# A kernel whose whole order is a table of words: the same steps in another order

## The chip, the cores and the metric

The kernel runs on one core of a Trainium2 chip. Five engines work side by side, each strictly in its own order: TensorE (PE; its weight loads are a row of their own, PEld), VectorE (DVE), ScalarE (ACT), GpSimd (POOL), and SyncE (SP), which here only issues transfers to the 16 DMA engines. The metric is the time of one execution on the device in microseconds (us). Three runs of the kernel before gave 236.62, 237.85 and 238.53 us; the median is 237.85.

## The reference

Two stages in a row, in float32 at the outside. The first is attention over 8 batches, 8 heads, 576 tokens and 64 numbers a head: a coarse attention over means of four tokens, and a local one in a band of three tokens to each side. The second mixes tokens and channels.

```python
q_d = q.reshape(B, H, Sd, factor, D).mean(axis=3)      # k_d, v_d likewise; factor 4
out_up = np.repeat(sm_attn(q_d, k_d, v_d), factor, axis=2)
mask = np.abs(pos[:, None] - pos[None, :]) < factor
out_local = softmax(where(mask, scale * q @ k.T, -1e9)) @ v
x = out_up + out_local                                  # as [batch, token, 512]
theta = x @ w_theta
zr, zi = x * cos(theta), x * sin(theta)
y = einsum('ts,bsd->btd', w_tok_r, zr) + einsum('ts,bsd->btd', w_tok_i, zi)
u = x + y
return u + maximum(u @ w_ch, 0.0)
```

## The kernel before

Batches run one behind the other, but several are under way at once: while one batch is mixed over its tokens, the next is in its attention, and the loads of later ones are on their way. Every batch goes through steps with names of two letters, and a step is a few instructions on one engine.

- Loads, issued by SP into 16 staging slots of 128 x 576 float32: lk and lq (two heads of k or q each, L287), lv and lw (two halves of a v chunk, 64 rows with 256-byte pieces, L348), la, lb, lc (theta, token and channel weights, L240 to L257). ck, cq, cv, ca, cb and cc cast them to bfloat16 (L296, L396, L243, L261).
- Attention: tp transposes q and k on PE (L303), ev brings them from PSUM (L316), kd and qd are sums of four tokens (L322 to L336). pv and vd make the coarse v (L404, L412, L415). sd, ed, nd, xn, xd and xc are the coarse attention. ps are the local scores (L482), ex their exponentials (L490), mk the band (L501), po the product with v (L511), nm the division (L519, L520), xt the turn to channels by tokens (L533), xa the sum with the coarse part into xT (L541).
- Mixing: th and tt are theta (L552, L564), cs and ct its cosine and sine on ACT (L557 to L570), xm turns x back (L591), zz multiplies (L616), zt with zp and zc or with a transposing transfer dz handles the last 64 tokens. mx multiplies by the token weights, nine products for each of eight pieces of a batch (L632), and ua adds x (L637). The token weights themselves are transposed once on PE (wp, L273) and brought back (wc, L278).
- Output: ch is the channel product (L662), up and uc, or the transposing transfer du (L641), turn u to tokens by channels, rl adds and clips (L667), st stores (L671). The last 64 tokens of two batches go together: ut, dt, ht, rt, and the tail stores ss and sr (L700).

For batches 6 and 7 the transposes xm are transfers too (dx, L601), and for batch 7 those of k and q (dk, L307).

What sets the order is one long string, ORDER (L57 to L97). Each word is the next step of its kind; the letters behind the name are the place: a PSUM bank or pair of banks, a staging slot, or the engine of a cast or an eviction (v DVE, a ACT, g POOL). A word wm is a stretch of warm-up products (L755), on zeros, whose result nobody reads. te and ts load ACT's tables. The loop at L749 walks the string, and pin() ties each instruction to the one ahead of it on its engine, so each engine's order, SP's queue included, is the string's:

```python
for word in ORDER.split():
    kind, place = word[:2], word[2:]
    ...
    STEPS[kind][0](*next(todo[kind]), place)
    pin()
```

Waits between engines follow from the data: a step waits for what it reads, for its bank, slot or buffer to be free, and a load also for the landing of the eighth load ahead of it.

Of the kernel before, what the change touches and what calls it, by code (L numbers as in the profile page):

```python
# [58 lines left out]
lq9 x11 tp45 kcg cqa cva cqg x16 cqg lka cvv cvv lqb evv cvv ckg cva lkc kdg cka cqa lqd ckg lke laf wm772 tp23 evv
wm754 tp67 pv45 tp01 qdv kcg eva vdv la0 kdg lq1 eva cka wm256 ps23 ex ps67 lk2 qdv ps01 mkv wm446 sd45 sd23 ex ed  # L60
po67 ed cav cqg la3 po45 nm nm lk5 nd67 cqa xn mkg nd23 ex xn cag cka tp45 lq6 eva la4 po01 po67 lb8 nm lb9 xd2 wm303
tp45 lb7 cqa lba lqb ckg lbc lbe xcv mkg lbd lbf xt01 caa nm lb1 po23 kdg xa eva lv0 lv2 xt67 tp45 lw cag th0 lv5 cba
cbg lw cbg cqg lw xa xm1 nm th6 xt23 lv6 evv th7 ts cs xa zz tp45 cbg cbg wp0 cs wcv lv3 xm6 cs tt2 xm3 th7 wp1 lw xm0
zz zz lw qdv lk8 wcv eva ct lk4 lq9 cs cbg cbg cbg cbg wp6 wca wp3 wp2 wp4 wp5 wca wp1 wcv wcv wcv wp2 ztg ps67 ps45
qdg wcv te ex wcv ex lq7 kdg lkb lka zz lkc lqe lkd zp1 zcv cvv lqf mx3 cvg cvg cvg mkv ua cvg lq1 mx2 sd01 ps67 lv0
mkv lq2 ex po45 mx3 nm sd67 ua cqg po45 ed lw po01 nm ua nm mx2 ed ua pv67 po45 lq5 mx3 cqg vda nm nd01 ua cka up2
nd67 mkg cka xn ckg ckg lk6 uca xn up3 tp45 uca tp01 xd6 eva ckg xt23 mx7 xcv eva qdg xa xt45 po01 th6 cqg xa lv3 ckg
lv9 tp23 nm ts cs cqa th4 lq7 xm5 xt01 th6 evv cs tp23 xa zz cqa tt4 ua tp01 kdg cs ct cqg evv ztv th5 lw evv lw xm7
zz cs tp23 mx6 xm4 kdg zp5 qdg ua eva zz cvv ps01 cqa ps23 lv8 xm7 kdg zz zcv lk4 te ex lw mx6 mx4 ua mx5 sd01 mkv lvb
lw ua ex po67 mkv cva ps23 qdg lca lcc utg ed lce nm mx4 cvg ex lcd lvf ua lk1 po01 lk2 sd67 lw po23 ckg nm cqa nm mx5  # L70
ckg ed tp01 cvg ua lq5 eva tp67 mx4 lq0 cca ua up5 evv cvg ua ccg ccg pv23 mkg ucv vda lk3 qdv ps01 ps67 ex up4 mx5
ccv nd23 ex ua nd01 uca kdg ch5 po67 xn ps23 ckg cka lv9 mx4 xn tp01 lw ex mkg rl nm lk6 cva ckg xd5 sd23 ua cqg xcv
xt67 lv7 eva mx4 lw lv4 lw cvg xa lv8 lw ed xt01 po23 po67 th5 ua ch4 cqa ts cs xa nm nm th0 po23 lqb xt67 rl up1 cs
nm kdg th5 xm0 xa cs xm4 tp23 xm6 tt7 mkg cvg zz th0 lqc ucv zz st up1 cvg up5 ch4 eva ucv ckg ct ucv ch1 zz po23 cs
sd67 lve lva rl mkv te ed cvg pv45 lqd lk1 ztg cqg ch0 rl rl lk2 ch1 qdg nm lq3 vda tp67 nd45 rl cqa xm0 lqf eva lw zz
xn nd23 zp1 utg lw xn tp67 zca lk5 lq9 kdg mx0 up1 ua po45 lv0 eva ckg lk7 ps23 nm lw po67 nm ckg lv4 uca mx0 tp45 lk6
qdg mx1 ua xd0 ps67 ua lv8 ex eva xca ckg sd23 xt45 xa lw mx1 mkg st cvg ua ed mx0 ex mx1 mkv ua th0 po23 ua xt45 ts
cs xa xt67 mx1 xm0 xa th4 xm5 lqb zz ua tt0 kdg xm1 cvv ckg cvv th6 ch7 cqg cka cqg cs ct nm cs lvc cqg lk1 ztv tp23
eva lw th0 rl zz cs cqg zz tp67 evv cvg xm4 zz st zp5 zca ch1 rl cva tp23 mx0 po67 ua eva ps45 lw nm po23 lv2 te ex
lv5 mx1 pv67 lke cqg st mx0 po45 dt vda nm lk7 mkv st lqd po23 ckg ua ua qdg sd67 ch1 qdg nm nm ht0 cka ed rt lv3 up6  # L80
up7 cvg ucv uca nd45 kdg cqg nd23 mx0 xn lw xn ps67 ss ps45 ex ex xd2 mx3 tp67 xcv up2 cva ua uca tp45 lq6 rl evv up0
cqg lw eva ch1 ua lvf xt67 ps23 ucv sd45 xa cva st ex lw lq9 rl lk4 mx0 sd23 ed xt67 ua ckg xa lva qdg lw mkv kdv xt45
mx1 cvg th0 ua st lvb mx6 ua lw ed mkg tp23 ts cs utg lw mx7 cqg xa ua up6 po01 po45 cvg eva uca pv23 tt7 nm vda lq0
nm th6 xm0 zz nd45 ct cs ch1 lv1 xn cva st tp23 nd67 cva xn up0 th4 xm5 th6 zz sr eva xm7 xm5 ps23 lv8 lvc rl uca cs
po01 ch4 zz lw cs nm zz ztg ch7 te ex dz xd6 ch5 cvg rl lw lqe utg rl mkg po01 ps23 st mx4 lw lkd up7 cqg cka st ex
up2 uca nm ch3 rl xt01 kdg st st cvg xcv cva qdg ckg ua xa mkg uca po45 pv67 mx2 nm mx0 ua lk6 sd45 vda lk2 rl lq7
xt67 cqg ua ps23 xa mx1 lv5 ed po45 ua lq3 nm st mkv cqg dt ex dk9 sd23 xt67 ckg ed mx0 mkg du xa nd45 ch1 ckg ua po23
xn po67 th0 ts cs th4 tt5 nm cs nd23 rl dkf nm ct cqg evg dka xm1 xm0 mx6 zz th1 th7 cs dk1 cs xm4 xm5 zz ztv xn ua zz
mx6 zz mx4 po23 ua dz xt01 po67 xd5 ua xcv eva lw evg mx4 nm st mx5 eva du xa mx2 ht3 qdg ua mx4 xt01 ua kdg nm ua utg
ps67 du rt cvv du st ps23 kdg ua te ex ex mx5 mx4 ps67 lvb lv0 lw lw qdv xa lv8 sd23 cva xt01 ua mkv xa mkg mx5 ex st  # L90
lv4 ua po67 ua ed nm sd01 ed po23 mkg cvg ch4 ch5 mx0 nm tt1 lw lw cvg cvg rl sr po67 rl dxd po23 ua nm po45 nm ts ct
nm th0 pv67 th1 dx vda ch2 ztg nd45 st st nd67 du xn du xn cs cs du th3 cs th0 xd1 xt45 xt67 rl xcv cs xt23 xa utg dxc
ch1 dx zz ch0 ch4 xa ss ch5 dz th6 zz ch7 dt du xa tt2 zz th3 dxe dx zz st cs rl th1 mx6 cs mx3 ct st ua rl ztv rl cs
dx7 dx mx2 th6 ht4 rt zz mx1 ua mx0 cs rl mx3 mx6 zz dz rl zz ua ua zz mx7 mx1 mx2 ua ua mx0 ua mx3 ua mx6 ua ua mx1
st ua du mx0 st mx2 ua ss utv ch3 ua ua ua st ua utv ch2 ch1 ch0 ch7 ch6 du ch4 du du du du st rl sr rl du du rl dt
ch1 st st rl st rl st st rl rl ht0 rl st st rm su rt sr ss st
# [702 lines left out]
```

## Time and profile before

| What | Value |
|---|---|
| time, median of three runs | 237.85 us (236.62 to 238.53) |
| span of the profiled execution, first to last instruction | 232.1 us |
| mean granted TensorE clock in it | 0.997 |
| DMA queue of the program, share of 16 engines | 84.6% |
| bytes moved, mean rate | 49.41 MB, 213 GB/s |

For the profiled execution the page gives the span alone; what lies around a span is in the runs' times and not in the page. Its busy table gives each engine's busy time, its share and its instructions. The slices cut the span in 40 equal parts of 5.8 us; a digit is the busy share in tenths. Rows of a group read: line, engine, operation, out<-in, size, count | busy us, mean ns of one | idle us ahead of them and who ended it. Rows of the timeline begin with start and duration in us. Rows of waits read: who waited <- for whom: us in total, times, longest.

### The profile page before, as it was taken

The page shows a single profiled execution, that of the slowest core. Times are in us where ns is not written, and L with a number is a line of the kernel's source. Part 1 is how long each engine was busy: PE and PEld are TensorE (multiplying, and loading weights), DVE is VectorE, ACT ScalarE, POOL GpSimd, SP SyncE. Part 2 cuts the span into 40 slices and gives each one's busy share as a digit, 9 for nine tenths or more (in the row PEclk, how much of TensorE's full clock was granted, in tenths as well). Part 3 has the DMA queues.
Part 4 walks back from the last instruction along what each step waited for, and adds up shares of the span by engine and source line. Part 5 has one row for each costly group of instructions (what it writes and reads, how often), then busy time and mean ns, then how long its engine had stood idle before and what let it go on. Part 6 is the DMA issues. An engine that isn't in the chain of part 4 may idle for free.

```text
span 232.1 us, 9462 instructions
## 1 busy us (share of the span) xinstructions
PE 220.7 (95%) x3986; PEld 153.2 (66%) x3986; DVE 191.8 (83%) x365; ACT 156.1 (67%) x241; POOL 135.5 (58%) x179
## 2 busy tenths in 40 slices
PE   7998899999998999999999999999999998999991
PEld 2665678777776765776768766676676563767750
DVE  6699999989997988868997997799889967567572
ACT  3359999799877989867976979857766591620000
POOL 7468989869999656897472837767386510000000
PEclk9999999999999999999999999999999999999998
DMA  6999989999999899989606895899957766556676
GB/s 204 382 392 390 298 134 252 365 263 193 264 263 195 224 290 208 203 209 210 174 3 178 226 234 147 293 249 173 153 122 189 144 138 100 154 126 182 138 235 217
DMA packets 76795, 49.41 MB, mean 213 GB/s; under 512 B 61136, under 2 KB 61392, under 8 KB 76752
## 3 DMA queue, kind: packets, MB, share of 16 engines
q1 hardware_dynamic: 76752, 48.81, 84.6%
q8 instruction: 31, 0.51, 1.1%
q14 instruction: 12, 0.10, 0.2%
HBM read 33.98 MB, written 9.44 MB: 187 GB/s over the span
## 4 chain that ended last, share of the span: by engine, by line
PE 72%; DVE 12%; DMA 5%; SPq 3%; issue 3%; ACT 2%; DVEq 0%
PE PS L632 24%; PE PS L662 10%; PE PS L552 9%; PE PS L303 5%; PE PS L755 4%; PE PS L511 3%; DVE xT L541 3%; DMA out_dram<-osb 2%; DVE pm L501 2%; PE PS L591 2%; PE PS L482 2%; DMA st<-xT 2%; SPq L641 2%; PE PS L533 2%; DVE uT L637 2%
## 5 line engine op out<-in xcount | busy, mean ns | idle before, releaser
L632 PE MATMUL PS<-WT,z 128*128 128x288 bf16 x576 | 77.9, 286 | 1.7 <-issue 1.7
L632 PEld LDWEIGHTS <-z 128*128 128x128 bf16 x576 | 53.8, 98 | 17.5 <-issue 2.8
L637 DVE TENSOR_TENSOR uT<-PS,xT 128x288 bf16<-128x288 f32 x64 | 28.1, 450 | 11.4 <-PE PS L632 11.1
L552 PE MATMUL PS<-wth,xT 128*128 128x512 bf16 x128 | 32.3, 380 | 0.7 <-DVE xT L541 0.7
L557 ACT ACTIVATE cs<-PS,pihc 128x512 bf16<-128x512 f32 x32 | 22.3, 696 | 15.1 <-PE PS L552 9.9
L662 PE MATMUL PS<-wch,uT 128*128 128x512 bf16 (+1 forms) x132 | 30.6, 373 | 0.0
L520 DVE TENSOR_TENSOR tmp<-PS,rl 128x512 bf16<-128x512 f32 x40 | 27.7, 692 | 1.4
L541 DVE TENSOR_TENSOR xT<-PS,xdT 128x928 bf16<-128x928 f32 (+1 forms) x24 | 22.7, 952 | 3.4 <-PE PS L533 3.1
L490 ACT ACTIVATE pm<-PS 128x1024 bf16<-128x1024 f32 (+1 forms) x24 | 20.4, 877 | 7.0 <-PE PS L482 2.7
L501 POOL TENSOR_TENSOR pm<-pm,band 128x1024 bf16<-128x1024 bf16 (+1 forms) x13 | 22.2, 1709 | 2.9 <-ACT pm L490 2.9
L667 DVE SCALAR_TENSOR_TENSOR osb<-PS,ur 128x512 f32<-128x512 f32 (+1 forms) x33 | 21.8, 669 | 2.4 <-PE PS L662 1.6
L330 POOL TENSOR_TENSOR two<-kT 128x580 f32<-128x580 bf16 x15 | 17.5, 1163 | 6.1 <-ACT kT L316 5.2
L296 POOL CAST q_tm<-st 128x576 bf16<-128x576 f32 x22 | 14.4, 664 | 10.8 <-DMA st<-in_q_dram 10.8
L662 PEld LDWEIGHTS <-uT 128*128 128x128 bf16 x132 | 12.2, 98 | 12.2 <-issue 0.3
L558 ACT ACTIVATE cs<-PS 128x512 bf16<-128x512 f32 x32 | 19.4, 605 | 0.0
L330 POOL TENSOR_TENSOR two<-qT 128x576 f32<-128x576 bf16 x11 | 12.8, 1167 | 10.5 <-ACT qT L316 7.1
L552 PEld LDWEIGHTS <-xT 128*128 128x128 bf16 x128 | 11.2, 98 | 10.7 <-issue 1.3
L616 DVE TENSOR_TENSOR z<-PS,cs 128x1024 bf16<-128x1024 bf16 x24 | 16.2, 685 | 1.9 <-PE PS L591 0.9
L437 ACT ACTIVATE pd<-PS 128x864 bf16<-128x864 f32 x16 | 14.1, 889 | 5.2 <-PE PS L426 5.2
L761 ACT ACT_TABLE_LOAD x13 | 16.7, 1283 | 0.2
L296 POOL CAST k_tm<-st 128x576 bf16<-128x576 f32 x21 | 14.4, 695 | 1.4 <-DMA st<-in_k_dram 1.4
L396 POOL CAST v_w<-st 128x512 bf16<-128x512 f32 x21 | 13.3, 653 | 1.3 <-DMA st<-in_v_dram 1.2
(119 smaller groups left out, 419.3 us busy)
## 6 DMA issues: line engine op xcount, KB each, us to landing
st<-in_q_dram SPq DMA_DIRECT2D x32, 288.0 KB, 6.3
st<-in_k_dram SPq DMA_DIRECT2D x32, 288.0 KB, 6.0
st<-in_v_dram SPq DMA_DIRECT2D x70, 128.0 KB, 4.7
out_dram<-osb SPq DMA_DIRECT2D x31, 256.0 KB, 2.9
out_dram<-osb SPq DMA_DIRECT2D x10, 128.0 KB, 2.4
st<-in_v_dram SPq DMA_DIRECT2D x4, 288.0 KB, 3.7
st<-in_moe_w_tok_r_dram SPq DMA_DIRECT2D x4, 288.0 KB, 6.2
st<-in_moe_w_tok_i_dram SPq DMA_DIRECT2D x4, 288.0 KB, 7.2
```

Source lines behind the costliest of these rows:

```text
L296: COPY[w](out=to[:, r, :], in_=of[:, r, :])
L330: nc.gpsimd.tensor_tensor(out=t, in0=src[:, :, 0:2], in1=src[:, :, 2:4], op=ALU.add)
L490: nc.scalar.activation(out=pm[(3 * b + u) % NPM][:, :, 0:n].rearrange("p e c j w -> p e (c j w)"), in_=at.pop(("ps", b, u))[:, :, 0:4 * W ...
L501: EW[w].tensor_tensor(out=t, in0=t, in1=m, op=ALU.mult)
L520: nc.vector.tensor_tensor(out=tmp[(NCH * b + c) % NTMP].rearrange("p g (j d) -> p g j d", d=D), in0=ps[:, :, :, 0:D], in1=r.unsqueeze(3).t ...
L541: nc.vector.tensor_tensor(out=xT[b % 2][:, :, lo:lo + cnt].rearrange("p e (m j) -> p e m j", j=4), in0=at.pop(("xt", b, u))[:, :, 0:cnt].r ...
L552: nc.tensor.matmul(out=ps, lhsT=xT[b % 2][:, dc, P * c:P * c + P], rhs=wth[:, dc, :], start=(dc == 0), stop=(dc == 3))
L557: nc.scalar.activation(out=t[:, 0, :], in_=ps, func=AF.Sin, bias=pihc, scale=1.0)
L632: nc.tensor.matmul(out=ps, lhsT=z[b % 2][:, j, P * dc:P * dc + P], rhs=WT[:, j, cols], start=(j == 0), stop=(j == 8))
L637: nc.vector.tensor_tensor(out=uT[b % 2][:, dc, cols], in0=at.pop(("mx", b, i)), in1=xT[b % 2][:, dc, cols], op=ALU.add)
L662: nc.tensor.matmul(out=ps[:, cols], lhsT=uT[b % 2][:, dc, P * c:P * c + P], rhs=wch[:, dc, cols], start=(dc == 0), stop=(dc == 3))
L667: nc.vector.scalar_tensor_tensor(out=o[:, cols], in0=at["ch", b, c][:, cols], scalar=0.0, in1=ur[b % 2][:, c, cols], op0=ALU.max, op1=ALU.add)
```

## The change

All of ORDER is replaced, and nothing else. It has the same steps in another sequence, with other banks, slots and engines. The word k0, which does nothing, goes to the end. A line of the difference as an example, and the table's first line in both forms:

```diff
@@ -55,45 +55,45 @@
 ORDER = """
-l10 l11 l12 c1v c1a c1g k0 l13 kcv wm061 t101 c1g lq4 e1v wm256 t123 lk5 lk6 kca e1v wm483 x12 x13 lk7 ckv lq8 x10 cka
...
+l10 c1a l11 c1g l12 l13 wm7a5 t101 c1v c1v t123 lk4 kcg ckv lk5 lq6 lq7 kcg lk8 e1v e1a ckg lk0 kcg wm743 tp45 evv x10
...
 """
```

The words that differ in number or engine, before and after:

| Words | before | after |
|---|---|---|
| casts of k and q on DVE, ACT, POOL | 1, 20, 43 | 17, 12, 35 |
| evictions ev of k and q on DVE, ACT, POOL | 9, 21, 2 | 6, 22, 4 |
| sums kd and qd on DVE, POOL | 6, 26 | 3, 29 |
| band masks mk on DVE, POOL | 11, 13 | 8, 16 |
| coarse v evictions vd on DVE, ACT | 1, 7 | 4, 4 |
| evictions uc on DVE, ACT | 6, 10 | 10, 6 |
| casts of v on DVE, ACT, POOL | 8, 11, 21 | 5, 10, 25 |
| table loads te, ts | 6, 7 | 8, 9 |
| warm-up words and products | 8, 48 | 6, 28 |

Three places are shown. The first is SP's queue where the token weights are loaded (L253 to L257). `st` is the staging area; a row with x4 is four transfers. Before:

```order
L240 DMA st<-in_moe_w_theta_dram 128x512
L255 DMA st<-in_moe_w_tok_r_dram 128x576 x4
L287 DMA st<-in_q_dram 128x576
L253 DMA st<-in_moe_w_tok_r_dram 64x576
L253 DMA st<-in_moe_w_tok_i_dram 64x576
L257 DMA st<-in_moe_w_tok_i_dram 128x576 x4
L348 DMA st<-in_v_dram 64x8x64 x10
```

And the same place after the change:

```order
L255 DMA st<-in_moe_w_tok_r_dram 128x576
L348 DMA st<-in_v_dram 64x8x64
L255 DMA st<-in_moe_w_tok_r_dram 128x576
L253 DMA st<-in_moe_w_tok_r_dram 64x576
L253 DMA st<-in_moe_w_tok_i_dram 64x576
L257 DMA st<-in_moe_w_tok_i_dram 128x576 x3
L287 DMA st<-in_q_dram 128x576
L348 DMA st<-in_v_dram 64x8x64
L257 DMA st<-in_moe_w_tok_i_dram 128x576
L348 DMA st<-in_v_dram 64x8x64 x6
```

Three half-loads of v (the third stands a few rows higher, behind the first weight) now go ahead of the last token weight, where all ten stood behind it.

The second place is DVE's order while batch 2 is mixed: between pieces of the mix, which ua (L637, `uT`) ends, stand steps of batches 3 and 4. `tmp` is the divided local attention, `vd` the coarse v, `xT` the sum. Before:

```order
L541 TENSOR_TENSOR xT_102<-PS,xdT_100 128x4x232
L637 TENSOR_TENSOR uT_111<-PS,xT_101 128x288
L501 TENSOR_TENSOR pm_84<-pm_84,band 128x1024
L637 TENSOR_TENSOR uT_111<-PS,xT_101 128x288 x2
L541 TENSOR_TENSOR xT_102<-PS,xdT_100 128x4x232
L541 TENSOR_TENSOR xT_102<-PS,xdT_100 128x4x112
L616 TENSOR_TENSOR z_104<-PS,cs_105 128x1024
L637 TENSOR_TENSOR uT_111<-PS,xT_101 128x288
```

And after:

```order
L541 TENSOR_TENSOR xT_102<-PS,xdT_100 128x4x232
L637 TENSOR_TENSOR uT_111<-PS,xT_101 128x288
L541 TENSOR_TENSOR xT_102<-PS,xdT_100 128x4x232
L541 TENSOR_TENSOR xT_102<-PS,xdT_100 128x4x112
L412 CAST vd_72<-PS 128x8x64
L415 CAST vd_72<-PS 32x4x64 x2
L501 TENSOR_TENSOR pm_84<-pm_84,band 128x1024
L316 COPY kT_63<-PS 128x2x576
L457 RECIPROCAL rd_97<-PS 72x8
L458 TENSOR_TENSOR xdn_95<-PS,rd_97 72x512
L667 SCALAR_TENSOR_TENSOR osb_119<-PS,ur_114 128x512
```

Fewer pieces of the mix stand between the steps of the later batches, and the coarse v of batch 4, which ACT evicted, is on DVE here.

The third place is SP's queue near the end, where the transposes of batch 6 are transfers (L601 from `xT_101`) among those of u of batch 5 (L641 from `uT_112`) and the stores. Before:

```order
L348 DMA st<-in_v_dram 64x8x64 x3
L700 DMA out_dram<-osb_120 64x512
L601 DMA_TRANSPOSE st<-xT_101 128x4x128 x2
L671 DMA out_dram<-osb_121 128x512
L671 DMA out_dram<-osb_122 128x512
L641 DMA_TRANSPOSE ur_114<-uT_112 128x4x128 x3
L601 DMA_TRANSPOSE st<-xT_101 128x4x128 x2
L700 DMA out_dram<-osb_120 64x512
```

And after:

```order
L601 DMA_TRANSPOSE st<-xT_101 128x4x128
L700 DMA out_dram<-osb_120 64x512
L671 DMA out_dram<-osb_118 128x512
L671 DMA out_dram<-osb_119 128x512
L641 DMA_TRANSPOSE ur_114<-uT_112 128x4x128
L601 DMA_TRANSPOSE st<-xT_101 128x4x128 x2
L641 DMA_TRANSPOSE ur_114<-uT_112 128x4x128
L671 DMA out_dram<-osb_121 128x512
L601 DMA_TRANSPOSE st<-xT_101 128x4x128
```

The four transfers of batch 6 start earlier, with one of u between them at a time, and the last loads of v have moved far ahead.

At the very end of SP's queue the half-row store of the last chunk (L671) stood behind the two tail stores (L700); now it goes ahead of them.

More of the change, by code (lines that the diff above doesn't have):

```diff
@@ L57 @@
 ORDER = """
-l10 l11 l12 c1v c1a c1g k0 l13 kcv wm061 t101 c1g lq4 e1v wm256 t123 lk5 lk6 kca e1v wm483 x12 x13 lk7 ckv lq8 x10 cka
[L59 to L96, printed above, removed]
+l10 c1a l11 c1g l12 l13 wm7a5 t101 c1v c1v t123 lk4 kcg ckv lk5 lq6 lq7 kcg lk8 e1v e1a ckg lk0 kcg wm743 tp45 evv x10
@@ new lines @@
+cva x11 cqg x12 cva lq9 lqa cqg x13 kcv cva x16 cvv tp45 ckg la2 ckv cva wm730 tp23 pv01 eva eva cqv kdg cqv tp45 eva
+wm752 ps45 vdv lk1 lk3 ps01 qdg la4 caa ex ex kdv ckg ckv qdg wm716 tp23 sd45 lq5 sd67 lq6 lq7 mkv ed ed cqg po01 po45
+cqg nm nm mkg la8 lb0 nd67 cag lv9 eva nd01 ps23 caa tp45 lka lkb ex xn xn po67 po23 nm nm eva lbc xd0 xca ckg la2
+wm107 xt45 xa lb3 lv1 lb5 lb6 ckg tp67 mkg po23 cag lbd lbe lb8 xt01 th4 xa cba xm5 eva ts nm qdg cbv cs th0 lqa cs
+xt23 xa lvb lb4 cbg lv0 th1 cbg cbg cbg wp2 cqv zz lv2 xm3 zz th4 wcv lw lvf xm5 wp3 cbg wp0 cs cs tt2 ct xm1 cbg cqg
@@ new lines @@
+zz wcv wcv lw wp5 wca zz lw cbg wp4 tp67 ztv wp2 wcv wp1 wp5 kdg eva wcv qdg wcv wcv kdg wp4 wca te zp2 ps67 ps01 ps35
+cvg ex ex zcv lk8 lka lke cvv cvv ex mx2 ua mx4 lw cvg mx2 sd01 lq4 ed mkv ua lw sd67 po34 ed mkv cvg nm mx5 pv01 ckg
+cqg lqd ua vda ua lq7 lk6 lq5 po34 po67 nm nm mx2 ua ckg tp01 ckg nd34 cqa tp67 eva nd25 up0 up1 eva lc1 mkg lcb xn xn
+ckg ucv lvc lv3 uca tp34 eva po67 po25 cqg nm xd1 nm lk9 lk0 ccg mx0 xt34 xt67 xca lk2 lw lq4 lka cqa ts lvd ckg xt12
+xa xa xa lw mx5 th3 lv6 lv7 tp67 xm1 evv ua cs lv1 qdg tt2 ckv cvg cvg th4 xm3 xm6 th0 th7 ct kdg xm2 ua cs cs kdg
@@ new lines @@
+tp45 cqg cs te lq9 ckg ckg ztv zp0 zz zz lw lqe mx3 cqg zz ps67 ex cvg zcv lk5 lqf ps01 zz evv ua mx2 ua tp45 lc8 cqv
+qdg lqc lw lw lw tp67 lw cvg lv0 cvg lv4 lv2 mx2 ex cqv tp01 mkg mkv eva ccg cka evv up4 mx5 ua ua eva lka sd01 ed ucv
+sd67 po23 nm mx5 lk9 lk3 lke lkd lkf po23 ed cka ckv ua po01 lq6 lq5 pv67 vda up5 ccg uca nm nm mx4 ua kdg po67 nm
+ps23 ex qdg qdg cqa ps01 ex nd45 cka kdg nd23 cva mx6 tp01 lkb xn xn xd2 mkv lw lw lw mx3 xcv eva ps24 ps01 lca ccg
+lk9 ex ex mkg lv8 lvc lv3 mkg ua lq7 lqa po56 ch7 ua cqg sd24 nm cvg cva rl st ed cva ts lv0 cvg xt56 xt01 lq4 xa xa
@@ new lines @@
+mx7 xt56 po24 th3 cs lw lw lw xa th0 ckg lv1 lw lw up5 xm6 nm zz cka lkd ch2 lke cs pv34 ucv rl tt5 ct ckg up6 th0 ua
+cs th5 cqv ch7 vdv cvg cvg cs te lv5 ucv po06 sd34 ed ch2 ch5 rl ztv nm tp67 xm0 rl rl zp2 xm3 st st eva zz cvg tp45
+cvg eva nd01 xm6 ckg lqb lv0 lv3 zcv lvc up2 uca utv utv cqg zz dt ch7 lw tp45 nd23 lk7 lk8 zz xn eva rl st st xn mkv
+tp01 eva mx7 ps23 ex lw po01 po45 ua cqg cqv xd7 ht6 lqa nm xca ps23 lqf po07 lk2 nm lv4 lw ex mx1 nm xt23 lq6 ua kdg
+rt qdg kdg qdg sd07 kdg sd45 xa mx1 ua lw ed xt67 ed ts xt23 mkg xa xa cvg pv45 vdv mkv th1 cs tp67 eva th2 tt3 tp45
@@ new lines @@
+evv ckg nd01 xn ch6 th7 th4 ct cqa cs po01 po25 rl ztv cs ps36 cs qdg mx7 lq1 lq9 nm nm xm4 cqa te nd01 ua ckv zz mx2
+ua mx7 ex lqb xn up3 uca xm6 lqa tp01 eva mkg cka ckg cqg cqv mx2 zz ua ua xm7 xd6 xca xm0 lw zp2 zca po13 ss ps45 ex
+zz zz lvd lv6 lw qdg cvg cvg cqa cva up6 mx7 cva kdg lv7 cvg nm ch4 ua utv xt12 ucv lqf rl ps57 ex lve po36 nm mx0
+tp56 tp34 lw lw mx7 xa po12 ua mkg mkg ua eva nm eva ps56 ex mx0 qdv sd12 sd56 po34 ua ed ed ch7 up0 pv12 nm vda ucv
+xt56 mkg xt34 cqv cqg lv5 lv0 mx0 mx1 xa xa cka ts ckg up3 tt4 rl kdg ct cqv cqg tp67 eva cvv up5 lv3 ucv th2 cs ua
@@ new lines @@
+tp34 ucv ua nd67 evv th1 nd25 xn mx3 po67 cs te lvc lk1 xn ps14 lq4 ps25 ua xm3 nm mx0 zz kdg qdg ckg mx3 dk8 dka cqv
+po67 ua ua utv lkd ex ex ckg po25 po01 nm st mkg st nm nm cvg th4 lw lw lw lw cva ts cvg cvg cs th3 cs ch6 xd4 up2 st
+lv1 lvd st rl xt01 xca uca te sd35 xt67 ch4 ch2 xa xa xm0 xm1 zz ch6 ed mkg st rl st po03 ps57 ex ts lw zz th4 cs rl
+nm xm5 up7 th2 cs ucv up0 ch7 zz pv45 ztg dz ucv xm0 xm3 cvv mx1 zz zz ua vdv sr mx0 mx1 evg mx4 evg ua ua qdg ua up1
+uca te ch0 ch1 dka evg rl rl dk0 evg sd67 rl xt45 kdg cvg rl po23 xa mx0 ed ts tt4 nm kdv xm5 ct th6 ua cs ztg nd23 st
@@ new lines @@
+nd47 th0 lw lw cs te cvg xn ht2 xn xd4 zz po37 xcv nm ps56 ex po01 nm qdg dt dz mx4 xm3 mx7 du rt sr ua ps25 ex mkg
+po46 du mx0 zz xt23 ps15 ex nm ua xa ua sd47 st st du mx6 du ed xt23 xt45 sd07 mx1 mkg ed xa po07 mkg cvg po23 xa dx1
+utg cvg pv45 ss ua nm ua st th6 mx0 vda ts cs ua st mkv nm nd45 nd17 xn du mx0 mx6 mx4 dx dxd ua ua mx6 xn ua ua po14
+po07 po25 nm tt3 ct ztg du ch6 nm nm rl ch1 rl xd0 ch7 rl ch6 rl xca xt01 xt23 xt45 st th7 xa dx st st mx6 ua utv xa
+dz th0 th6 th1 dt cs zz zz cs xa cs th0 th6 tt4 ct th5 zz dxc dx cs cs ht2 dx3 zz cs mx4 mx1 ua mx4 mx6 ua du mx1 ua
@@ L97 @@
+ua dx zz ch6 ua ch1 du du ch4 ztv zz zz st cs dz zz mx5 mx0 ua rl rl rt ch5 du du rl sr mx1 mx2 mx4 mx6 ss mx3 rl st
+ua ua ua du ua ua mx6 mx4 du ua du utg mx3 st ua mx6 ch2 ch1 st ua ch4 ch0 st du ua ua rl rl rl rl du ch1 ch4 uta st
+st rl dt ch0 rl rl st st st ch1 st st rm su rl st ht4 rt ss sr k0
 """
```

## The prediction

> **What bounds the kernel now.** I read the page's busy table and its slices first, then the waits, then the stretches of time that the waits pointed to.
>
> ```profile
> span 232.1 us, 9462 instructions
> ...
> PE 220.7 (95%) x3986; PEld 153.2 (66%) x3986; DVE 191.8 (83%) x365; ACT 156.1 (67%) x241; POOL 135.5 (58%) x179
> ...
> PE   7998899999998999999999999999999998999991
> ...
> DMA  6999989999999899989606895899957766556676
> ```
>
> TensorE (PE) is busy 95% of the span, and its row has a digit under 9 only three times in the first five slices, twice in the middle and in the last. The DMA row has a 0 in slice 21, and PE still has a 9 there. The waits and a table of stretches say the same:
>
> ```profile
> SPq L700 <- DVE rd L457: 10.9, 1, 10.9
> DVE uT L637 <- PE PS L632: 11.1, 15, 2.4
> PE PS L632 <- issue: 1.7, 2, 1.1
> PE PS L552 <- DVE xT L541: 0.7, 1, 0.7
> ...
> core 0: us, PE busy (x) PEld busy (x) DVE busy (x) ACT busy (x) POOL busy (x), PEclk, DMA share, GB/s
> 2.00:24.00 22.00, 21.21 (x332) 12.65 (x333) 18.43 (x40) 12.48 (x20) 15.10 (x30) 1.00 1.03 371
> 28.00:32.60 4.60, 4.60 (x68) 2.96 (x67) 4.57 (x8) 4.59 (x9) 4.60 (x8) 1.00 1.03 172
> 116.00:122.00 6.00, 6.00 (x103) 3.88 (x101) 5.52 (x13) 4.56 (x9) 4.29 (x6) 1.00 0.01 3
> ```
>
> The load queue once stood 10.9 us behind a tail store (L700), so nothing was moved from 116 to 122 us, and PE was busy for all 6.00 us of it: loads run far enough ahead. DVE waits for PE's mixing product (11.1 us in all), while PE's own largest waits are 1.7 and 0.7 us. So PE sets the end, and a new order can win only in the start, in few and small PE waits, and in the tail.
>
> I split the span at the first mixing product (step mx of batch 0), the first PE step that needs every token weight. Ahead of it PE has the same steps in both kernels, save warm-up products and one more piece of scores (ps of batch 1); behind it the same steps in another order. The span is therefore the start of that product plus a rest that changes only by waits.
>
> ```profile
> 34.12 2.32 PE L273 MATMUL PS<-ident,uT 128*128 128x128 bf16 x40
> 36.38 0.72 PE L482 MATMUL PS<-qT,kT 64*64 64x64 bf16 x64
> 37.03 0.40 PE L583 MATMUL PS<-ident,zT 128*128 128x128 bf16 x4
> 37.26 1.51 PE L632 MATMUL PS<-WT,z 128*128 128x288 bf16 x11
> ```
>
> It starts at 37.26 us, so the rest is 232.1 - 37.26 = 194.8 us.
>
> **Term 1, the start: +0.6 us.** Two things pull against each other. First, 28 warm-up products stand where 48 stood, with 13,248 columns for 22,464.
>
> ```profile
> 14.43 1.19 PE PS L755 x6
> ...
> 16.16 1.12 ACT L316 COPY kT<-PS 128x1152 bf16<-128x1152 bf16 x1 [2.13 <-PE PS L303]
> ```
>
> The six in this chain row have 2,816 columns in 1.19 us, 0.42 ns each, so 9,216 fewer columns free 3.9 us of PE. What may use it is batch 0's attention: ScalarE waited 2.13 us for a transpose that stood behind warm-ups. I give PE 2.1 us of the 3.9; the rest would be waits, for the loads of batch 0 come no sooner. PE then reaches the first transpose that needs the imaginary weights (step wp of tile 1; it began 10 products into the x40 row, about 34.7) near 32.6.
>
> Second, those weights come later. In the new queue three half-loads of v stand ahead of the last weight load; before, all v stood behind it.
>
> ```profile
> 22.70 3.11 SPq L257 DMA_DIRECT2D st<-in_moe_w_tok_i_dram  x4
> 26.34 9.49 SPq L348 DMA_DIRECT2D st<-in_v_dram  x10
> ...
> st<-in_moe_w_tok_i_dram SPq DMA_DIRECT2D x4, 288.0 KB, 7.2
> ...
> 29.50 3.86 POOL L261 CAST uT<-st 128x576 bf16<-128x576 f32 x6
> ```
>
> The last weight was issued 0.33 us before the end of its row, at 25.5, and with 7.2 us to landing arrived about 32.7; POOL's six casts end at 33.36, so its own cast began then. Each half-load is 128 KB. At the 172 GB/s of 28.0 to 32.6 three take 2.3 us. At the least they add nothing: v loads were issued from 26.34 on and already shared the 16 engines with the last weights. I take 1.2, the middle, since the row lies between: landing 33.9, the cast 0.65, so 34.6 (PE waits 2.0 there). From this transpose to the first mix stand 30 weight transposes (2.26/40 us each: 1.70), nine of q (0.50), four of zT (0.23) and five units of scores (0.80): 3.2 us. The product starts at 37.9, 0.6 later than before. With the bounds of the landing it is 36.7 to 39.0: -0.6 to +1.7.
>
> [...]
>
> One unit of scores (0.14 us) moves from behind the product to ahead of it: **-0.1** on the rest.
>
> **Term 2, VectorE in the middle: +1.2 us.**
>
> ```profile
> 37.26:147.55 110.29, 108.30 (x2206) 78.38 (x2204) 96.04 (x176) 92.86 (x144) 82.01 (x101) 1.00 0.89 215
> ...
> 9.90 0.53 DVE L296 CAST k_tm<-st 128x512 bf16<-128x512 f32 x2
> 17.20 0.68 DVE L412 CAST vd<-PS 128x512 bf16<-128x512 f32 x1
> 17.80 0.84 DVE L415 CAST vd<-PS 32x256 bf16<-32x256 f32 x2
> ...
> L520 DVE TENSOR_TENSOR tmp<-PS,rl 128x512 bf16<-128x512 f32 x40 | 27.7, 692 | 1.4
> L541 DVE TENSOR_TENSOR xT<-PS,xdT 128x928 bf16<-128x928 f32 (+1 forms) x24 | 22.7, 952 | 3.4 <-PE PS L533 3.1
> L316 DVE COPY kT<-PS 128x1152 bf16<-128x1152 bf16 x6 | 8.1, 1352 | 0.3 <-PE PS L303 0.3
> ```
>
> From the first mix of batch 0 to that of batch 4 (37.26 to 147.55) DVE is busy 96.0 of 110.3 us, 87%. Counted in the new order between the same two steps, DVE gains 11 casts of k and q (0.53 each), 2 evictions vd (1.4 with the three parts above), 3 nm (0.89 with their reciprocal), 2 xa (0.95), 4 uc and 6 smaller copies (about 3.3), and loses 2 masks, an eviction of k or q, a kd reduction, a cast each of v and of a weight, and 3 others (about 8): some 9 us more. PE gains there 2 th (0.86 each), 2 xm, 2 xt, 2 po, a pv and others: 4.0 us. So DVE has 105 us of work for 114.3 of PE, 92%; its 14.3 us of idle time must shrink to 9.2. If all of it does, the cost is 0. If DVE idles as long as before, the stretch takes 105.1 + 14.3 = 119.4, and 5.1 us are lost. Much of the old idle time is the wait for the mix (L637, 11.1 us over the span), which goes when DVE is late; so I take a quarter, 1.2. The cover of the added casts is this idle time and nothing else. What ScalarE and POOL give or take (POOL has most masks and sums, 58% busy) lies beside PE work.
>
> **Term 3, late transfers: -1.0 us.**
>
> ```profile
> 184.78 3.84 SPq L641 DMA_TRANSPOSE ur<-uT  x3
> 188.67 2.59 SPq L601 DMA_TRANSPOSE st<-xT  x2
> ...
> 189.98 3.98 DMA st<-xT
> 194.65 1.13 DVE xT L541
> 195.82 1.02 PE PS L552 x4
> ```
>
> In the chain the third transposing transfer of batch 6 waits on SP behind three of uT (3.84 us) and lands at 193.96; DVE's sum follows, then PE's theta product, which waited 0.7. In the new queue one uT transfer stands ahead of it, 2.6 us less, and the v loads of batch 7 are out of the way. The 0.7 goes, and I add 0.3 for the short PE wait at 135 us that followed the 10.9 us stop of the queue. Bounds: 0 (another chain is just behind) to -1.5. If late transfers don't matter even so, term 3 is 0.
>
> **Term 4, the tail: -0.6 us.**
>
> ```profile
> 227.08 0.69 DVE osb L695
> ...
> 227.80 1.12 SPq L700 DMA_DIRECT2D out_dram<-osb  x2
> 228.97 0.59 SPq L671 DMA_DIRECT2D out_dram<-osb  x1
> ```
>
> PE ends on the same product ht. Behind it three stores were issued, the last at 228.97; now the half-row store goes ahead, and the two tail stores are the last: one issue of 0.59 us less. Bounds: -0.6 to 0.
>
> **Sum.** +0.6 - 0.1 + 1.2 - 1.0 - 0.6 = +0.1, a span of 232.2. The page gives no time for its execution but the span; the median of the runs is 5.75 above it, which I take as what lies around it: 237.95, say 238.0. The three runs reach from 236.62 to 238.53, so the profiled execution may stand 1 us away from the median.
>
> **Rivals.**
> - *The start or the middle comes out at its good end.* Weights land no later (-0.6), DVE's added work is all covered (0), late transfers give 1.5: -0.6 - 0.1 - 1.5 - 0.6 = -2.8, 235.0. For it: PE was busy through a 6 us stop of transfers, so slack is there. Against: a weight behind three more loads must not be late. 23%.
> - *VectorE becomes the bound* between the mixes of batches 0 and 4: +0.6 - 0.1 + 5.1 - 1.0 - 0.6 = +4.0, 241.9. It decides when DVE's idle time in that stretch stays over 9.2 us. For it: 92% load in a fixed order, where each wait for a bank is passed on to PE. Against: the old waits L637 are cover. 29%.
> - *The new places of transfers give nothing*: term 3 is 0 and the time is 239.0. For it: the 10.9 us stop. 7%.
> - *PE goes cold.* The chain shows what a slow start costs:
>
> ```profile
> 1.26 2.74 PE PS L226 x6
> ```
>
> Six products of 512 columns took 2.74 us, 0.89 ns a column where later ones take 0.42; a second such stretch costs 1.4 us, 239.4. It needs an idle PE; the wait that I see is 2.0 us. 3%. [...]
>
> **How the numbers follow.** My forecast has the other 38%. About 1% (2.4 us) is what a measurement of this kernel can tell from no change. Forecast, the useless transfers and the cold PE end within it: 48%. Faster by more: 23%, slower by more: 29%. The range reaches from a little under the first rival to the second: 234.0 to 242.0.
>
> **What would show it.** The profile after should have the first mix at 37.9 with an idle PE (about 2 us) just ahead of the odd weight transposes; DVE busy 92% between the mixes of batches 0 and 4, its wait L637 well under 11.1 us; no wait of theta on L541 near the end; the end 4.5 us after PE's last product. I am wrong if the first mix starts before 36.7 or after 39, or if PE waits for DVE in the middle for more than 2.4 us.

## The result, and the profile after

The changed kernel takes 278.94 us (median of 4 runs, 278.36 to 280.99) where the kernel before, beside it, takes 238.19. The ratio is 1.174 (95% interval 1.167 to 1.182). Forecast were 238.0 us, and 242.0 at the upper end of the range. Each ratio in this document compares undisturbed executions of both kernels, taken side by side; the median beside it is of all executions.

The profiled execution has a span of 277.3 us for 232.1. The span grew by 45.2 us and the median time by 40.8, because the profiled execution before was a short one: 1.8 us lie around the span after (279.08 us in all), so a span of 232.1 belongs to some 234 us, and not to the median of 238.

The page after, its head, busy table and three of its slice rows; a slice is now 6.93 us:

```profile
span 277.3 us, 9423 instructions
...
PE 232.2 (84%) x3966; PEld 157.4 (57%) x3966; DVE 199.3 (72%) x398; ACT 154.7 (56%) x232; POOL 146.5 (53%) x183
...
PE   8878997998986888778989858999665969989992
...
PEclk9979997999999899999999997999977799999999
...
DMA  7999999999899994992692880480351514464597
```

PE stands idle for 277.3 - 232.2 = 45.1 us; before it was 232.1 - 220.7 = 11.4. That is 33.7 of the 45.2 us that the span grew; the other 11.5 are busy time of the same work. The loss is in no one place: PE's row has a digit under 9 in 24 of its 40 slices, all over the run, where it was 7 before. And no other engine took over as the bound, since each of them has a smaller share than before.

Who makes PE wait? The largest rows of PE in the view of waits after (who <- for whom: us, times, longest):

```profile
PE PS L511 <- ACT pm L490: 4.8, 3, 2.3
PE PS L552 <- DVE tmp L520: 2.5, 3, 1.0
PE PS L632 <- ACT pm L490: 2.2, 1, 2.2
PE PS L662 <- DVE tmp L520: 2.0, 2, 1.1
```

Three of these four rows make no sense by the data. Theta (L552) reads xT and a weight, the channel product (L662) reads uT and a weight, the mix (L632) reads z and the token weights; none reads an exponential (L490) or a divided local product (L520). What is left is the bank, and only one of these six waits, of L662, was for a bank that the eviction really holds. The mix is the clearest case, in the timeline after:

```profile
40.03 1.28 PE L632 MATMUL PS<-WT,z 128*128 128x288 bf16 x9
...
41.07 2.41 ACT L490 ACTIVATE pm<-PS 128x1024 bf16<-128x1024 f32 x3
...
43.52 1.75 PE L632 MATMUL PS<-WT,z 128*128 128x288 bf16 x11 [2.22 <-ACT pm L490]
```

The first piece of batch 0 (word mx2, bank 2) runs at 40.03. The second (mx4, bank 4) waits 2.2 us, until the third exponential of batch 1 is done. That exponential empties the scores of the word ps35, that is banks 3 and 5. It holds neither bank 4 nor anything that the mix reads. Bank 4 only lies between.

In the kernel before, every two-bank tile is on neighbouring banks. In the changed one 33 of 150 are not: 9 at distance 2, 15 at 3, and 9 at 4 to 7, all in ps, po, sd and nd. The function pair (in the listing) makes one view of both, `PS[:, a:b + 1:b - a, :]`. In the trace after, 14 PE steps start just behind an eviction of a pair that encloses their bank and does not hold it; they waited 15.3 us. Such a wait is called false from here on. In the trace before there is none. The evicting engines are hit too, where a bank of theirs lies between two of another's view or the other way round: 13 steps of VectorE waited falsely for 19.8 us and 7 of ScalarE for 18.9. One of these, in the view of waits after:

```profile
ACT pd L437 <- DVE uT L637: 4.6, 1, 4.6
```

This is the exponential of the word sd07, in banks 0 and 7. Up to 119.89 us it waits for VectorE to read bank 1, which is none of its own, and the next step of PE in bank 6 (xt67) waits 1.5 us for it in turn. Another 19 waits of PE for evictions, 15.7 us, were for banks that are really shared; a false wait ahead of such an eviction makes it late.

### The profile page after: what moved, and what is told of

Read it like the earlier page. It is cut to its first block, busy times and chain, and to the rows that moved or that the text cites. A ratio compares the mean times of both kernels' runs of the same rounds, so it can differ in the third digit from the quotient of the medians.

```text
span 277.3 us, 9423 instructions
## 1 busy us (share of the span) xinstructions
PE 232.2 (84%) x3966; PEld 157.4 (57%) x3966; DVE 199.3 (72%) x398; ACT 154.7 (56%) x232; POOL 146.5 (53%) x183
## 4 chain that ended last, share of the span: by engine, by line
PE 49%; DVE 22%; DMA 13%; ACT 6%; issue 6%; SPq 2%; POOL 1%; DVEq 0%; ACTq 0%; POOLq 0%
PE PS L632 19%; PE PS L662 6%; PE PS L552 5%; DMA st<-in_v_dram 4%; DVE tmp L520 4%; DMA st<-in_moe_w_ch_dram 3%; DVE xT L541 3%; PE PS L303 3%; ACT pm L490 3%; PE PS L755 3%; DMA st<-in_q_dram 2%; DVE q_tm L296 2%; DVE uT L637 2%; ACT pd L437 2%; DMA st<-xT 2%
## 5 line engine op out<-in xcount | busy, mean ns | idle before, releaser
L632 PE MATMUL PS<-WT,z 128*128 128x288 bf16 x576 | 81.5, 295 | 3.0 <-ACT pm L490 2.2
L632 PEld LDWEIGHTS <-z 128*128 128x128 bf16 x576 | 55.7, 100 | 19.9 <-issue 4.1
L637 DVE TENSOR_TENSOR uT<-PS,xT 128x288 bf16<-128x288 f32 x64 | 28.6, 452 | 24.1 <-PE PS L632 21.4
L501 POOL TENSOR_TENSOR pm<-pm,band 128x1024 bf16<-128x1024 bf16 (+1 forms) x16 | 29.4, 1845 | 13.4 <-ACT pm L490 13.4
L552 PE MATMUL PS<-wth,xT 128*128 128x512 bf16 x128 | 33.6, 399 | 3.0 <-DVE tmp L520 2.5
L662 PE MATMUL PS<-wch,uT 128*128 128x512 bf16 (+1 forms) x132 | 31.5, 376 | 5.2 <-DVE tmp L520 2.0
L490 ACT ACTIVATE pm<-PS 128x1024 bf16<-128x1024 f32 (+1 forms) x24 | 20.5, 881 | 15.1 <-PE PS L482 9.5
L520 DVE TENSOR_TENSOR tmp<-PS,rl 128x512 bf16<-128x512 f32 x40 | 27.6, 691 | 1.4
L330 POOL TENSOR_TENSOR two<-qT 128x576 f32<-128x576 bf16 x15 | 17.3, 1151 | 14.5 <-ACT qT L316 14.1
L437 ACT ACTIVATE pd<-PS 128x864 bf16<-128x864 f32 x16 | 13.7, 888 | 17.4 <-PE PS L426 6.9
L662 PEld LDWEIGHTS <-uT 128*128 128x128 bf16 x132 | 12.4, 99 | 16.1 <-issue 5.1
L552 PEld LDWEIGHTS <-xT 128*128 128x128 bf16 x128 | 11.9, 101 | 15.3 <-issue 5.2
L511 PE MATMUL PS<-v_w,pm 64*64 64x65 bf16 x640 | 11.9, 197 | 10.0 <-ACT pm L490 4.8
L396 POOL CAST v_w<-st 128x512 bf16<-128x512 f32 x25 | 15.2, 619 | 8.8 <-DMA st<-in_v_dram 8.6
L519 DVE RECIPROCAL rl<-PS 128x8 f32<-128x8 f32 x40 | 8.1, 202 | 16.0 <-PE PS L511 7.5
L330 POOL TENSOR_TENSOR two<-kT 128x580 f32<-128x580 bf16 x14 | 16.2, 1160 | 4.2 <-ACT kT L316 3.9
```

Of the source, the lines that this page charges most:

```text
L330: nc.gpsimd.tensor_tensor(out=t, in0=src[:, :, 0:2], in1=src[:, :, 2:4], op=ALU.add)
L490: nc.scalar.activation(out=pm[(3 * b + u) % NPM][:, :, 0:n].rearrange("p e c j w -> p e (c j w)"), in_=at.pop(("ps", b, u))[:, :, 0:4 * W ...
L501: EW[w].tensor_tensor(out=t, in0=t, in1=m, op=ALU.mult)
L520: nc.vector.tensor_tensor(out=tmp[(NCH * b + c) % NTMP].rearrange("p g (j d) -> p g j d", d=D), in0=ps[:, :, :, 0:D], in1=r.unsqueeze(3).t ...
L552: nc.tensor.matmul(out=ps, lhsT=xT[b % 2][:, dc, P * c:P * c + P], rhs=wth[:, dc, :], start=(dc == 0), stop=(dc == 3))
L632: nc.tensor.matmul(out=ps, lhsT=z[b % 2][:, j, P * dc:P * dc + P], rhs=WT[:, j, cols], start=(j == 0), stop=(j == 8))
```

## The experiments

### First guesses: engines, loads, casts

My first suspects were those that the prediction had named: VectorE's casts of k and q, and the places of the loads. Four kernels set them apart. They change only words of ORDER.

```diff
 e1: the new order and banks, engines of all casts, evictions, sums and masks as before (117 words)
-wcv wcv kdg wp4 wca te zp2 ps67 ps01 ps35 cvg
+wcv wcv kdg wp4 wcv te zp2 ps67 ps01 ps35 cvv
 e2: the old order and banks, the new engines (the same 117 places)
 e3: the new order, loads sorted by their casts, slots dealt anew
-ex ex zcv lk8 lka lke cvv cvv ex mx2 ua mx4 lw
+ex ex zcv lw lk6 lq7 cvv cvv ex mx2 ua mx4 lk8
 e4: the new order, 17 casts of k and q from VectorE to ACT
-ckv cqv
+cka cqa
```

> The new order with every cast, eviction, sum and mask on the engine that the old one gave it; banks, slots and sequence stay new. Casts theory (the 17 casts of q and k on VectorE take 0.9 to 1.2 us where 0.53 was counted, about 10 us of VectorE, and its lateness goes to TensorE): 279 falls to 255-268. Loads theory (the new queue asks for loads long before they are needed, while transfers are saturated): stays within 276-282. Order theory (the new sequence and banks make TensorE, VectorE and ScalarE wait for each other): 272-284.

Measured: 306.18 us, 1.289 of before (1.273 to 1.304), 27 us above the changed kernel. No theory expected more than 284.

> The old order with the engines of the new one. Casts theory: 238 rises by 10 or more, to 248-262. Loads theory and order theory: 236-243.

Measured: 253.56 us, 1.067 (1.053 to 1.081). The casts theory alone had this (248 to 262), but it had e1 wrong by 38 us. The new engines cost 16 us in the old order, and the old ones 27 in the new. Each order is slower with the other's engines, so neither swap says which half of the change lost the time.

> The new order; at the places of its loads in the queue the loads stand sorted by the place of their cast, and the staging slots are dealt out anew for that; all else stays. Before the first channel product 19.7 MB then have to be loaded instead of 22.5 (18.0 in the old order). Loads theory: the 11 us that TensorE was late there mostly go, and some that follow from them: 255-268. Casts theory and order theory: 275-282.

Measured: 276.83 us, 1.165 (1.146 to 1.185), beside 1.174 for the changed kernel: nothing that can be told apart.

> The new order with only the 17 VectorE casts of q and k moved to ScalarE (56% busy). Casts theory: 255-268. Loads theory: 275-282, order theory 272-284.

Measured: 280.25 us, 1.180 (1.163 to 1.196): nothing gained. Neither the loads' order nor the casts alone hold this kernel. What e1, e3, e4 and the changed kernel share is the new sequence and its banks.

### Banks: neighbouring or apart

Now the timeline at 43.5 us gave the theory of the span: a view over two banks that lie apart is waited for as if it held the banks between as well. Three kernels change the bank digits alone, and a fourth the loads too. One rule deals the banks in all: the bank that has been free for longest by ORDER, with the distance of each pair given.

```diff
 e5: the new order, all pairs neighbouring
-wp4 wca te zp2 ps67 ps01 ps35 cvg
+wp0 wca te zp7 ps34 ps12 ps56 cvg
 e6: the old order, the 33 pairs as far apart as in the changed kernel
-mx2 sd01 ps67 lv0 mkv lq2 ex po45
+mx0 sd12 ps57 lv0 mkv lq2 ex po34
 e7: the old order, all pairs neighbouring (a control)
-mx2 sd01 ps67 lv0 mkv lq2 ex po45
+mx0 sd67 ps34 lv0 mkv lq2 ex po12
```

> The changed kernel with only its PSUM banks dealt anew: the same sequence of steps, engines, staging slots and loads, and every two-bank tile on two neighbouring banks (33 of the 150 lie apart in the changed kernel: 9 at distance 2, 15 at 3, 9 at 4 to 7). The theory of the span: a view over two banks that lie apart is waited for as if it held the banks between as well, so that steps wait for evictions of banks that they do not use. It expects 238 to 258, the stalls that no step's own banks or data explain (27 us of PE time) nearly gone. The theory of the sequence (the new order itself leaves PE waiting, whichever banks it uses) expects 272 to 284.

Measured: 259.58 us, 1.101 (1.093 to 1.109): 19 us less than the changed kernel, and 1.6 above what the theory of the span allowed.

> The kernel before with only its PSUM banks dealt anew, so that the same 33 steps as in the changed kernel (of ps, po, sd and nd) have two banks at the same distances apart; order, engines, slots and loads are those of before. The theory of the span: 255 to 285, with PE stalls behind evictions of banks between. The theory of the sequence: 236 to 242.

Measured: 281.97 us, 1.195 (1.187 to 1.204).

> A control: the kernel before with its banks dealt anew by the same rule as in the other two, all pairs neighbouring. Both theories: 236 to 242, since no false wait is added and the order is the same; well above that would mean that the dealing itself costs time.

Measured: 250.94 us, 1.063 (1.055 to 1.072). This missed: the dealing itself costs 6%. I take it that this is because it goes by the place in ORDER and not by when a bank really comes free; no run shows that. So e5 and e6 are to be read beside e7, and not beside the kernel before.

The head and PE's busy time of e6, and then of e7:

```profile
span 279.7 us, 9454 instructions
...
PE 230.0 (82%) x3986; PEld 157.3 (56%) x3986; DVE 193.5 (69%) x365; ACT 157.0 (56%) x241; POOL 135.0 (48%) x179
```

```profile
span 250.5 us, 9474 instructions
...
PE 223.3 (89%) x3986; PEld 154.7 (62%) x3986; DVE 192.5 (77%) x365; ACT 156.6 (63%) x241; POOL 135.8 (54%) x179
```

Old order, old engines, old loads; the difference between the two is the distance of 33 pairs (and the other banks that this leads to). PE's idle time is 49.7 us in the one and 27.2 in the other, and the time differs by 31 us. By the test above e6 has 39 false waits, 15 of them PE's with 18.6 us, and e7 has none. With its pairs apart the old kernel is as slow as the changed one, though some 15 us of that are the dealing.

> Neighbouring banks for all pairs as in the first of these, and the loads also issued in the order in which their casts come. If the span was the loss and the loads' new order costs a few us beside it: 1 to 6 us under the first of these, 234 to 255. The theory of the sequence: 270 to 284. If loads are hidden once the banks are free: the same as the first of these within 1 us.

Measured: 256.99 us, 1.089 (1.079 to 1.099), 2.6 us under e5: as the first theory has it, though the intervals overlap and the time lies 2 us above its range.

### The same banks, without the span

Banks dealt anew change true waits too. A cleaner cut leaves every bank where it is and takes away the view over both. PE writes each bank by itself anyway. Only the eviction reads both in one instruction; here the 33 evictions of pairs that lie apart are made one bank at a time:

```diff
+SPLIT = {("nd", 1, 1), ..., ("sd", 7, 1)}
+    def banks(kind, b, i):
+        return (0, 1) if (kind, b, i) in SPLIT else (slice(0, 2),)
...
     def ex(b, u, w):
-        nc.scalar.activation(out=pm[(3 * b + u) % NPM][:, :, 0:n].rearrange("p e c j w -> p e (c j w)"),
-                             in_=at.pop(("ps", b, u))[:, :, 0:4 * W * n], func=AF.Exp, scale=SCL)
+        to = pm[(3 * b + u) % NPM][:, :, 0:n].rearrange("p e c j w -> p e (c j w)")
+        of = at.pop(("ps", b, u))[:, :, 0:4 * W * n]
+        for y in banks("ps", b, u):
+            nc.scalar.activation(out=to[:, y], in_=of[:, y], func=AF.Exp, scale=SCL)
```

The same is done in ed, xn and nm. e9 is the changed kernel with it, e10 the kernel before (same steps, a control), e11 is e6 with it, and e12 is e9 with the loads of e3.

> The changed kernel with order, engines, slots, loads and banks as they are; only the 33 evictions of a pair of banks that lie apart (ex, ed, nm, xn) are each issued as two instructions, one for each bank, so that no view spans a bank of another step. The split has a price of its own, some 0.2 to 0.4 us more of ACT or DVE for each, 7 to 13 us over the run beside other work. The theory of the span: 242 to 262, the waits of PE for evictions of banks between gone, and mx01 (bank 4) no longer behind the exponential of banks 3 and 5 at 43.5 us. The theory of the sequence: 277 to 290, since work was only added.

Measured: 252.06 us, 1.068 (1.059 to 1.076): 27 us less, with work added. By the rows of e9 two halves of an exponential take 2 x 0.596 us where the whole takes 1.017, and two halves of a division with their reciprocals 2 x (0.424 + 0.173) for 0.691 + 0.199: 0.2 to 0.3 us more. By the test above no false wait is left on any engine.

> A control: the kernel before with the evictions of the same 33 steps in two instructions each, all pairs neighbouring as before. It gives the price of the split alone: 237 to 246 by both theories.

Measured: 237.85 us, 1.006 (1.001 to 1.011): the split costs about 1 us, with VectorE busy 5.3 us more than before (197.1 for 191.8) and ScalarE 0.7 (156.8 for 156.1). So smaller evictions by themselves gain nothing.

> The kernel before with its banks dealt anew so that the 33 pairs lie apart (282.0 in its run), and those 33 evictions in two instructions. The theory of the span: back to what dealing anew costs by itself (250.9 with all pairs neighbouring) and the price of the split, 248 to 262. If the distance itself cost the time (the matmuls or the evictions being slower over banks apart): 278 to 292.

Measured: 257.19 us, 1.089 (1.082 to 1.095), 25 us under e6. The pairs still lie apart, so the distance itself is not slow. Over e7 with the price of the split (1.069) two points are left, which I can't place; the banks of e7 and e11 aren't the same.

The timeline of e9 at the place that was shown above:

```profile
39.73 3.48 PE L643 MATMUL PS<-WT,z 128*128 128x288 bf16 x27
...
40.77 2.47 ACT L500 ACTIVATE pm<-PS 128x1024 bf16<-128x1024 f32 x4
```

L643 is the mix and L500 the exponential in this kernel, whose lines stand lower. Three pieces of the mix run as one, while ACT is still at the exponentials that the second piece waited for. The wait is not the chip's doing: it is in the program. These are rows of the two programs as built, and not of a trace: the same instructions of PE in the changed kernel and in e9, with the place among its weight loads and products first. 1314 is the last product of the first piece, 1316 the first of the second:

```
1314 L632 MATMUL PS_61<-WT_125,z0_103 128x288 [waits Activation_49]
1315 L632 LDWEIGHTS z0_103
1316 L632 MATMUL PS_61<-WT_125,z0_103 128x288 [waits Activation_49]

1314 L643 MATMUL PS_61<-WT_125,z0_103 128x288 [waits Activation_49]
1315 L643 LDWEIGHTS z0_103
1316 L643 MATMUL PS_61<-WT_125,z0_103 128x288
```

The wait of row 1316 for ACT is gone with nothing changed but the evictions' views. So whatever places the waits takes a stepped view for the whole stretch that it spans.

PE's many short gaps could be read as a shortage of banks. But e9 has the same tiles in the same banks and is 27 us faster, so for the larger part banks were not short; they were held in name.

> The first of these with the loads issued in the order in which their casts come. If the loads are late once the false waits are gone: 2 to 8 us under the first of these. If not: within 2 us of it.

Measured: 246.25 us, 1.043 (1.035 to 1.052), 6 us under e9. The engines' shares in the chain that ended last say the same, of e9 and then of e12:

```profile
PE 37%; DMA 21%; DVE 19%; issue 7%; POOL 6%; SPq 5%; ACT 2%; DVEq 0%; POOLq 0%
```

```profile
PE 47%; DVE 21%; DMA 13%; POOL 7%; issue 6%; SPq 3%; ACT 1%; DVEq 0%; POOLq 0%
```

In e3 the same edit had gained nothing that could be told from no change. It may be that a late load was hidden there behind a step that stood waiting for a bank anyway; but e3's interval (1.146 to 1.185 beside 1.174) is wide enough to hold the same gain, so this is not shown. Once the false waits are gone, the gain is clear.

### What is left

e12 is 4.3% above the kernel before, with 0.6 of it for the split evictions. Two kernels look for the rest in the engines.

```diff
 e13: e12, and the 17 casts of k and q from VectorE to ACT
-ckv cqv
+cka cqa
 e14: e12, and the engines of before at all 117 places
```

> The changed kernel with the 33 evictions by bank and the loads by need (246.3 in its run, 8 us over before), and the 17 casts of q and k that it gives to VectorE on ACT instead. If the casts on VectorE are what is left (VectorE late, its casts 0.90 to 1.19 us each and the transposes of q and k behind them): 238 to 243. If not: 244 to 252.

Measured: 249.75 us, 1.053 (1.042 to 1.063): nothing gained.

> The same two edits, and for all casts, evictions, sums and masks the engines of the kernel before (117 words). In the changed kernel with its false waits these engines cost 27 us more. If the split of the work between the engines is what is left: 237 to 244. If the new order is fitted to its own engines, so that the old ones come late at other places: 248 to 270.

Measured: 269.83 us, 1.145 (1.138 to 1.153): worse by 24 us.

So neither edit shows the casts or the new division of the work as the cause of the last 3 to 4%; the new order runs worse with the old engines. By the trace of e12, PE is idle for 23 us in short and many waits. Twelve of them, 7.1 us, are for VectorE's evictions of banks that are really shared, and five, 4.9 us, for its casts of k and q, whose move to ScalarE gained nothing. Whether another choice of those banks would take waits away wasn't tried, and this part stays open. No version here beats the kernel before.

In points of the time before: the changed kernel is 17.4 above it. Evictions by bank take 10.7 of that although they cost 0.6 themselves, so the false waits are worth about 11.3, or 27 us. The loads' order is worth 2.4, or 6 us, with those gone. About 3.7 are the rest of the new order.

## Why the prediction was wrong

**What failed is a term that is not in the sum.** The prediction says that the rest of the run, behind the first mix, "changes only by waits", and then prices only waits for VectorE's load (term 2) and for late transfers (term 3). The new PSUM banks, which the change names, got no price at all. I took it that a step waits for its own bank and no other, as the text ahead of the prediction has it, and never asked which banks a pair's view spans, although ps35 stands in the new ORDER and pair() in the listing. By the rows 1316 above a step can wait for every bank between the two of a view. e9 puts 27 us on that. None of the rivals was this mechanism; the range could not hold it.

**"PE sets the end, loads run far enough ahead."** This held for the kernel before. It was read as a property that the new order would keep, and it did not: PE's share fell from 95 to 84%, and the loads' places cost 6 us with the false waits gone (e12 against e9). (PE's row before has a digit under 9 three times in the middle, and not twice as I read it.)

**Term 1, the start: +0.6 us forecast, +2.8 measured.** The first mix starts at 40.03 for 37.26, beyond my upper bound of 39, and the way there is not the forecast one. The rows of POOL and PE in the timeline after, and two of PE's rows of waits:

```profile
35.21 0.67 POOL L261 CAST uT<-st 128x576 bf16<-128x576 f32 x1 [0.20 <-DMA st<-in_moe_w_tok_i_dram]
...
36.33 0.72 PE L273 MATMUL PS<-ident,uT 128*128 128x128 bf16 x10
```

```profile
PE PS L303 <- DVE k_tm L296: 1.6, 2, 1.2
PE PS L303 <- DVE q_tm L296: 1.1, 1, 1.1
```

The cast of the last weight does wait for its transfer, and begins at 35.21 where I had 33.9. But PE did not wait for it. The transpose that needs it is the sixth of the row at 36.33, at 36.6 where I had 34.6, and no idle time stands ahead of that row, where I had 2.0 us. PE came late by itself. Between 14 and 18 us it waited 2.7 us for VectorE's casts of k and q. Six of VectorE's 17 casts stand ahead of the first mix, where one stood before, and term 1 has no price for them. Right behind these waits, from 17.3 to 20.7 us, the granted clock is 0.50, where it was 1.00 before. So the 2.1 us that fewer warm-up products were to give to PE were not gained: its idle time ahead of the first mix is 6.2 us for 3.0. (By its own terms the sum gives 34.6 + 3.2 = 37.8, and not 37.9.) In the run as a whole term 1 is 2 of 41 us.

**Term 2, VectorE in the middle: +1.2 us, and the rival in which it becomes the bound (+5.1).** Stretches of time, columns as in the prediction; first the changed kernel from its first mix of batch 0 to that of batch 4, then e12 between the same steps:

```profile
40.00:181.30 141.30, 119.67 (x2349) 83.35 (x2338) 108.44 (x211) 100.32 (x149) 96.25 (x107) 0.96 0.82 189
```

```profile
41.10:165.40 124.30, 115.11 (x2344) 81.63 (x2337) 114.21 (x233) 99.69 (x159) 97.20 (x108) 1.00 0.82 210
```

In the changed kernel VectorE is busy 108.4 of 141.3 us, 77%, less than the 87% before, and its waits for the mix grew where I said that they would shrink from 11.1 us:

```profile
DVE uT L637 <- PE PS L632: 21.4, 22, 3.8
```

So the rival did not happen: VectorE was held up with PE. Without the false waits (e12) it does come to the forecast 92%, 114.2 of 124.3 us, though with more work than the 105 us that I had counted (the split evictions are part of it, and the casts below). Even then taking 17 casts from it gained nothing (e13).

**Term 3, late transfers: -1.0 us.** Theta of batch 6 no longer waits for the sum of the transfers' chain, as forecast. It waits for a division instead:

```profile
214.19 1.86 PE L552 MATMUL PS<-wth,xT 128*128 128x512 bf16 x4 [1.02 <-DVE tmp L520]
```

It uses bank 6, and the division empties po07 in banks 0 and 7. The 0.7 us that went came back as 1.0 of the false kind.

**Term 4, the tail: -0.6 us.** The last sum and the last issue in the timeline after:

```profile
272.48 0.69 DVE L695 SCALAR_TENSOR_TENSOR osb<-PS,utr 128x512 f32<-128x512 f32 x1
273.47 1.14 SPq L700 DMA_DIRECT2D out_dram<-osb  x2
```

277.3 - 272.48 is 4.8 us, for 232.1 - 227.08 = 5.0 before: -0.2 of the -0.6. The half-row store does go ahead, and the last issue ends at 274.61, 2.1 us behind the start of that sum for 2.5 before; what then lies up to the end is 2.7 us for 2.5.

**The time around the span.** I took 5.75 us for it, the median less the profiled span. The executions on record show 1.7 to 2.0 (279.08 us for a span of 277.3). This did no harm to the forecast, which comes out as the median plus 0.1.

**"PE goes cold", 3%.** It came, as a consequence. Three stretches of the changed kernel:

```profile
180.00:201.00 21.00, 18.64 (x320) 13.22 (x318) 16.12 (x33) 11.64 (x18) 14.06 (x12) 1.00 0.43 93
201.00:222.00 21.00, 15.81 (x242) 10.34 (x240) 9.01 (x19) 6.24 (x10) 2.93 (x4) 0.76 0.42 94
222.00:250.00 28.00, 23.30 (x292) 14.46 (x291) 16.08 (x32) 9.80 (x19) 1.15 (x1) 1.00 0.40 82
```

From 201 to 222 us the granted clock is 0.76: in the trace it is 0.50 from 205.1 to 208.5 and from 211.9 to 218.7 us, and 1.00 in between. From 208.5 to 211.8, ahead of the longer stretch, PE was busy for 1.5 of 3.3 us, with waits of 1.0 us at most; in the 3.4 us ahead of the shorter one, and ahead of each of the four earlier stretches at 0.50 (from 17.3, 44.6, 89.0 and 167.5 us), it was busy for 0.8 to 1.6. No single wait of PE in the run is longer than 2.4 us, so it was waits of the size of my 2.0 us, several in a row, that stood ahead of it. A slow stretch did not follow each time: from 223.5 to 226.9 PE was busy for 1.2 us, and the clock stayed at 1.00. In the trace before, where PE waited less, it is 1.00 up to PE's last product; in e9 its mean is 0.986, for 0.956 in the changed kernel. A mixing product takes 329 ns on the mean from 201 to 222 us, and took 286 over the whole run before; first after, then before:

```profile
L632 PE MATMUL PS<-WT,z 128*128 128x288 bf16 x56 | 9.6, 329 | 0.0
```

```profile
L632 PE MATMUL PS<-WT,z 128*128 128x288 bf16 x576 | 77.9, 286 | 1.7 <-issue 1.7
```

Over the run PE is busy 11.5 us more for the same steps and 20 warm-up products fewer; in e9, where the waits are gone, it is 222.7 us, 2.0 more than before. So most of these 11.5 us come with the false waits. I had priced a slow stretch at 1.4 us.

## What to carry to other kernels

Before a new assignment of buffers is priced, write out for each view the addresses from its first to its last element, and treat everything in that stretch as taken: a stepped view over two banks may hold those between. When an engine waits for an instruction whose output it does not read, ask for the shared buffer first; if there is none, look at the stretch that the views span. And a loss that is passed on through a fixed order may hide others behind it, so an edit that gains nothing that can be told (the loads, e3) is worth another try once the larger loss is gone.
